# Attention's first four blocks normalized after the value product, first sequence scored from plain float32, half the filler products

## The chip, the core and the metric

The program runs on one core of a Trainium2 chip. Its metric is the device time of one execution in microseconds (us). The core has five engines with a queue each: PE (TensorE, matrix products), ACT (ScalarE), DVE (VectorE), POOL (GpSimd) and SP (SyncE, which here only issues transfers). An engine takes its instructions in the order in which the compiler has put them and waits on semaphores for the others. PE's loading of the stationary operand is listed apart, as PEld.

## The reference

Three stages in float32, each fed by the one before:

```
# attention: B=2 sequences, H=8 heads, S=768 tokens, D=64; 4 sink tokens, window 128
scores = q @ k.T / sqrt(D)
keep   = (key is one of the first n_sink) | (0 <= query - key < window)
a      = exp(scores - max);  a = a / (sum(a) + 1e-9);  x = a @ v       # 1536 tokens x 512
# gated MLP, d_ff = 1536 (weights given as float64)
g = x @ w_gate;  x = (g / (1 + exp(-g)) * (x @ w_val)) @ w_out
# mixture of 8 experts, top 1, with a skip test
out = x;  for tokens with x @ w_skip > 0:  out += gate * relu(x @ w1[e]) @ w2[e]
```

## The kernel before

The 1536 tokens are 12 blocks of 128 (`n` = 0 to 11; six to a sequence, `i = n % 6`). Attention goes by block and by pair of heads (`pr` = 0 to 3, `j = 4n + pr`), because a query block sees only its own and the previous block of keys, and the four sinks. For each pair:

- `step_a`: PE transposes keys and queries into PSUM (`tqk`), ACT copies them into `kq` as float32r, a reduced float32 that PE multiplies in one go (the high half), and DVE subtracts to get what is missing (the low half, `lo_of`, line 71). On a sequence's first block POOL copies the sinks' keys beside them.
- `step_b`: PE makes the scores of two heads, each from three products (high by high, high by low, low by high, line 276; each head uses its own 64 rows of the array). DVE merges the two key blocks with a predicated copy (line 281), adds the mask and takes the maximum (line 286); ACT does exp with the sums (line 290); DVE adds 1e-9 and inverts (lines 291 and 292); DVE scales one head's probabilities and ACT the other's (line 297, and `act_copy` on line 68). DVE copies out the sinks' columns (`psk`, line 300).
- `step_d`: PE transposes the probabilities, ACT copies them out (`pt`), POOL cuts the two triangles.

For each block, `step_s` transposes the sinks' probabilities (`tsk`) and `step_e` sums values times probabilities in PSUM (`xps`, lines 350 and 358). ACT and DVE then write the result as high and low halves (`xt`), the MLP's input.

The MLP takes groups of four blocks. `mlp` runs over 12 chunks of 128 columns of d_ff: gate and value products (`gv`, line 462), tanh, multiply, and the down product (`acc`, line 474). Its weights come as float64. A transfer brings 512 KB into one of three buffers `st`; ACT and DVE turn it into float32, two operations each (lines 134, 135, 139, 140); ACT, with DVE or POOL, splits it into high and low halves (`ring`). There are 36 such conversions, three to a chunk.

The generator `attention` gives out these steps one by one. The first four blocks are drawn by the loop quoted below; it adds, at each of some 56 pulls, filler products on a dead tile (line 428, bf16, 256 columns) at a low priority, and conversions at a rate of six over the loop. The first four phases of the MLP then draw the remaining blocks between their own pieces: phase 0 (blocks 0 to 3) draws blocks 4 to 7.

```
    while done < GS:
        done = next(at)
        pulls += 1
        filler(2)
        while converted[0] < 6 * pulls // 56:
            convert_w()
```

The order on each engine is not the order of the code: a scheduler in the compiler orders instructions by priority and by its own estimate of when their inputs are ready, so conversions and filler products fall wherever it sees an engine free. PSUM pools bound how far the steps run ahead, two buffers each: `accp` holds the scores of the first four blocks, `attp` the transposed keys and queries, `gvp` the transposed probabilities (and later `gv`), `acqp` the sinks, `xps` and the filler's tile.

Of the kernel before, what the change touches and what calls it, by code (L numbers as in the profile page):

```python
# [8 lines left out]
F32 = mybir.dt.float32  # L9
# [4 lines left out]
ALU = mybir.AluOpType  # L14
# [4 lines left out]
def build(ctx: ExitStack, tc: tile.TileContext, q, k, v, n_sink, window,  # L19
# [14 lines left out]
    GB = 2  # L34
    PHASES = [(0, 0, GS, 0, NFC, 2 * GS), (1, 0, GS, 0, NFC, 3 * GS)]
# [138 lines left out]
    def make_masks():  # L174
        parf = const.tile([P, 4], F32, name="parf")
        pneg = const.tile([P, 2], F32, name="pneg")
        ks = const.tile([P, 4], F32, name="ks")
        kt = const.tile([P, 4], F32, name="kt")
# [45 lines left out]
    kq = {(hl, pr): att.tile([P, PW], F32R, name=f"kq{hl}{pr}") for hl in range(2) for pr in range(NPAIR)}  # L224
    vsk = [None] * B
    prob, psk, pt, xt, skt = {}, {}, {}, {}, {}
# [20 lines left out]

    def step_a(j):

        n, pr = divmod(j, NPAIR)  # L250
        i = n % NBLK
        t = attp.tile([P, 512], F32, tag="att", name="tqk")
        for a, src in enumerate((kb[n], qb[n])):
            nc.tensor.transpose(out=t[:, a * P:(a + 1) * P], in_=src[:, 2 * pr:2 * pr + 2, :].rearrange("p h d -> p (h d)"), identity=ident)
        o = (i % 2) * W
        src = t[:, 0:2 * P].rearrange("p (a f) -> p a f", a=2)
        hi, lo = (two(kq[hl, pr], o, KW - o) for hl in range(2))
        act_copy(hi, src)
        lo_of(lo, src, hi)
        if i == 0:  # L260
            for hl in range(2):
                c_ = nc.gpsimd.tensor_copy(kq[hl, pr][:, P:W], kq[hl, pr].bitcast(F32)[:, 0:4])
                begun.setdefault("POOL", c_.ins)

    def step_b(j):
# [7 lines left out]
        for m, (a, c) in enumerate(((0, 0), (0, 1), (1, 0))):  # L273
            for h in range(2):
                r = slice(64 * h, 64 * h + 64)
                m_ = nc.tensor.matmul(out=ss[h][:, 0:nk], lhsT=kq[a, pr][r, KW:PW], rhs=kq[c, pr][r, 0:nk], start=m == 0, stop=m == 2)
# [7 lines left out]
        st = sm.tile([P, 4], F32, tag="st", name="st", bufs=3)  # L284
        for h in range(2):
            r_ = nc.vector.tensor_tensor_reduce(out=p[:, h], in0=ss[h][:, odd * P:odd * P + W], in1=mk, scale=-0.125, scalar=3.0e38,  # L286
                                           op0=ALU.add, op1=ALU.min, accum_out=st[:, h:h + 1])
            begun.setdefault("DVE", r_.ins)
        for h in range(2):
            nc.scalar.activation(out=p[:, h], in_=p[:, h], func=ACTF.Exp, scale=-1.0, bias=st[:, h:h + 1], accum_out=st[:, 2 + h:3 + h])  # L290
# [50 lines left out]
    def step_e(n):  # L341
# [20 lines left out]
        hi, lo = (xt[g][a][:, :, u * P:(u + 1) * P] for a in range(2))  # L362
        act_copy(hi, x)
# [766 lines left out]
    while done < GS:  # L1130
        done = next(at)
        pulls += 1
        filler(2)
# [72 lines left out]
```

## Time and profile before

| what | value |
|---|---|
| three runs | 633.27, 635.26 and 635.63 us, median 635.26 |
| profiled execution | 634.08 us, of which the span of instructions is 632.3 us |
| busy share of the span | PE 93%, PEld 75%, DVE 71%, ACT 59%, POOL 30% |
| mean granted TensorE clock | 0.978 of 2.4 GHz |

The span is what the trace covers; the rest of an execution lies around it. The shares are means over very different stretches: in the first 73 us attention's first four blocks run with little product work, and from there to the experts at the end the MLP keeps PE filled. PE's share also contains the filler products. The chain that ended last holds only the last transfer and so tells nothing about the stage that the change touches; the stretches have to be looked at one by one.

### The profile page before, as it was taken

How to read it: one execution, taken by the hardware profiler on the slowest of the kernel's cores; microseconds unless marked ns; L12 is line 12 of the kernel's file. 1: busy time of each engine (PE TensorE's matmuls, PEld its weight loads, DVE VectorE, ACT ScalarE, POOL GpSimd, SP SyncE). 2: the span in 40 equal slices, each digit the busy share in tenths (PEclk: the TensorE clock that was granted, in tenths of full speed). 3: DMA queues.
4: the chain of work that ended last, by engine and by line, in shares of the span. 5: the costliest groups of instructions: out<-in, count | busy, mean ns of one | idle time of the engine just before them, and what ended most of it. 6: DMA issues, size and time to landing. Idle time of an engine off the chain costs nothing. (4 is left out here: it accounts for less than half of the span.)

```text
span 632.3 us, 10773 instructions
## 1 busy us (share of the span) xinstructions
PE 590.3 (93%) x3449; PEld 474.3 (75%) x3449; DVE 451.4 (71%) x1149; ACT 370.8 (59%) x872; POOL 191.0 (30%) x279
## 2 busy tenths in 40 slices
PE   5889898899999999999999999999997999999993
PEld 3666676668777877777778999899985777777762
DVE  4999889895555585665654577688747697879961
ACT  5788787786545454544553456657615674856730
POOL 4443254465433041101111030021005343537411
PEclk9889998999999999999999999999998999999997
DMA  8668976653010220100004200022108786978901
GB/s 208 147 186 228 259 215 181 200 168 67 0 35 2 84 51 17 36 5 14 1 0 155 96 30 1 1 87 92 33 35 243 250 259 199 338 223 267 345 2 37
DMA packets 78420, 75.81 MB, mean 120 GB/s; under 512 B 43138, under 2 KB 55426, under 8 KB 78352
## 3 DMA queue, kind: packets, MB, share of 16 engines
q1 hardware_dynamic: 75552, 69.32, 36.5%
q0 software_dynamic: 2512, 5.68, 2.7%
q8 instruction: 31, 0.51, 0.3%
q14 instruction: 37, 0.30, 0.2%
q10 hardware_dynamic: 288, 0.00, 0.0%
HBM read 65.37 MB, written 11.98 MB: 122 GB/s over the span
## 5 line engine op out<-in xcount | busy, mean ns | idle before, releaser
L462 PE MATMUL gv<-xt,ring 128*128 128x512 f32 (+1 forms) x1152 | 226.2, 345 | 1.6 <-ACT xt L68 0.8
L462 PEld LDWEIGHTS gv<-xt,ring 128*128 128x128 f32 x1152 | 176.0, 189 | 27.7 <-ACT xt L68 1.1
L68 ACT ACTIVATE ring<-w 128x512 fp32r<-128x512 f32 x144 | 90.3, 629 | 98.0 <-PE gv L462 70.4
L71 DVE TENSOR_TENSOR ring<-w,ring 128x512 fp32r<-128x512 f32 x108 | 74.6, 692 | 41.6 <-ACT ring L68 41.1
L71 DVE TENSOR_TENSOR w<-stage,w 128x512 fp32r<-128x512 f32 x96 | 87.4, 942 | 9.6 <-ACT w L68 7.5
L474 PE MATMUL acc<-ring,hh 128*128 128x512 f32 x288 | 92.5, 402 | 0.0
L68 ACT ACTIVATE w<-stage 128x512 fp32r<-128x512 f32 x128 | 72.9, 626 | 11.9 <-DMA stage<-in_moe_w_dram 8.7
L71 POOL TENSOR_TENSOR ring<-w,ring 128x512 fp32r<-128x512 f32 x36 | 48.5, 1349 | 54.2 <-ACT ring L68 54.1
L321 POOL TENSOR_SCALAR_AFFINE_SELECT pt<-pt 128x256 f32<-128x256 f32 x40 | 19.8, 495 | 138.1 <-ACT pt L68 138.1
L71 POOL TENSOR_TENSOR w<-stage,w 128x512 fp32r<-128x512 f32 x32 | 46.6, 1459 | 48.6 <-ACT w L68 27.0
L474 PEld LDWEIGHTS acc<-ring,hh 128*128 128x128 f32 x288 | 50.8, 188 | 10.8 <-ACT hh L68 0.6
L474 PE MATMUL acc<-ring,hl 128*128 128x512 f32 x144 | 57.2, 399 | 0.0
L290 ACT ACTIVATE p<-p,st 128x132 f32<-128x132 f32 x96 | 38.3, 400 | 31.1 <-DVE st L286 30.4
L877 PE MATMUL yps<-w,hT 128*128 128x512 f32 x192 | 47.1, 399 | 1.0 <-DVE w L71 0.6
L851 PE MATMUL hps<-w,xh 128*128 128x512 f32 x128 | 43.3, 418 | 0.7 <-issue 0.4
L877 PEld LDWEIGHTS yps<-w,hT 128*128 128x128 f32 x192 | 35.3, 188 | 10.4 <-ACTq L925 1.0
L497 DVE TENSOR_TENSOR th<-th,gv 128x512 f32<-128x512 f32 (+1 forms) x48 | 26.5, 552 | 20.7 <-PE gv L462 18.7
L645 POOL DMA_INDIRECT xs<-x,pi x12 | 13.2, 1103 | 81.2 <-ACT ring L68 48.6
L68 ACT ACTIVATE hh<-th 128x512 fp32r<-128x512 f32 (+1 forms) x48 | 25.1, 523 | 16.2 <-DVE th L497 15.7
L496 DVE SCALAR_TENSOR_TENSOR th<-th,gv 128x512 f32<-128x512 f32 (+1 forms) x48 | 26.3, 548 | 8.6 <-ACT th L493 8.6
L474 PEld LDWEIGHTS acc<-ring,hl 128*128 128x128 f32 x144 | 27.0, 188 | 7.0 <-DVE hl L501 0.4
L140 DVE SCALAR_TENSOR_TENSOR w<-w,st 128x512 int32<-128x512 int32 x36 | 30.8, 856 | 1.4
(171 smaller groups left out, 972.2 us busy)
## 6 DMA issues: line engine op xcount, KB each, us to landing
stage<-in_moe_w_dram SPq DMA_DIRECT2D x128, 256.0 KB, 4.5
st<-in_moe_w_gate_dram SPq DMA_DIRECT2D x12, 512.0 KB, 5.6
st<-in_moe_w_val_dram SPq DMA_DIRECT2D x12, 512.0 KB, 4.1
st<-in_moe_w_out_dram SPq DMA_DIRECT2D x12, 512.0 KB, 5.5
xs<-trash SPq DMA_DIRECT2D x8, 387.0 KB
qk<-in_k_dram SPq DMA_DIRECT2D x12, 256.0 KB, 3.9
qk<-in_q_dram SPq DMA_DIRECT2D x12, 256.0 KB, 3.7
vb<-in_v_dram SPq DMA_DIRECT2D x12, 256.0 KB, 3.7
```

The source lines that it names most:

```text
L68: nc.scalar.activation(out=out, in_=in_, func=ACTF.Copy, scale=scale)
L71: (eng or nc.vector).tensor_tensor(out=out, in0=in_, in1=hi.bitcast(F32), op=ALU.subtract)
L140: nc.vector.scalar_tensor_tensor(out=di, in0=di, scalar=3, in1=low, op0=ALU.logical_shift_left, op1=ALU.bitwise_or)
L290: nc.scalar.activation(out=p[:, h], in_=p[:, h], func=ACTF.Exp, scale=-1.0, bias=st[:, h:h + 1], accum_out=st[:, 2 + h:3 + h])
L321: nc.gpsimd.affine_select(out=d[:, 0], in_=d[:, 1], compare_op=ALU.is_ge, fill=0.0, base=0, pattern=[[0, 2], [1, P]], channel_multiplier=-1)
L462: nc.tensor.matmul(out=ps, lhsT=w_[:, kk * P:(kk + 1) * P], rhs=x_[:, kk, t0 * P:t1 * P], start=kk == 0 and m == 0, stop=kk == KD - 1 and ...
L474: nc.tensor.matmul(out=acc[g, t], lhsT=h_[:, s], rhs=w_, start=c == 0 and m == 0, stop=c == NFC - 1 and m == 2)
L496: nc.vector.scalar_tensor_tensor(out=th, in0=th, scalar=1.0, in1=gp, op0=ALU.add, op1=ALU.mult)
L497: nc.vector.tensor_tensor(out=th, in0=th, in1=vp, op=ALU.mult)
L645: d = nc.gpsimd.indirect_dma_start(out=xs[:, :], out_offset=bass.IndirectOffsetOnAxis(ap=pi[:, t], axis=0), in_=x2s[t], in_offset=None, bo ...
L851: nc.tensor.matmul(out=ps[half], lhsT=x_[:, kk, :], rhs=w_[:, kk, :], start=kk == 0 and m == 0, stop=kk == KD - 1 and m == 2)
L877: nc.tensor.matmul(out=y, lhsT=h_[:, c, :], rhs=w_[:, c % 4, :], start=c == 0 and m == 0, stop=c == NF2 - 1 and m == 2)
```

## The change

For blocks 0 to 3 (`n < LATE_SUM`) the probabilities stay unscaled. The sums of all heads of a block go into one tile, which DVE inverts once, after the last pair. In `step_e` PE spreads the inverses over 64 rows each (eight float32 products by the identity, `rps`, in a `gvp` buffer), ACT copies them out (`rs`), and DVE multiplies the block's result by them before it is split into halves. For blocks 0 to 5 (`whole(n)`, the first sequence) ACT's copy of keys and queries keeps full float32, there is no low half, and each head's scores are one float32 product. The loop for the first four blocks adds one filler product a pull. Four small constant tiles become one.

```diff
@@ make_masks @@
-        parf = const.tile([P, 4], F32, name="parf")
...
+        small = const.tile([P, 14], F32, name="small")
+        parf, ks, kt, pneg = small[:, 0:4], small[:, 4:8], small[:, 8:12], small[:, 12:14]
@@ step_a @@
+        if i == 0 and n <= NBLK:
+            new_kq(pr, [F32] if whole(n) else [F32R, F32R])
...
-        hi, lo = (two(kq[hl, pr], o, KW - o) for hl in range(2))
-        act_copy(hi, src)
-        lo_of(lo, src, hi)
+        if whole(n):
+            act_copy(two(kq[0, pr], o, KW - o), src)
+        else:
+            hi, lo = (two(kq[hl, pr], o, KW - o) for hl in range(2))
+            act_copy(hi, src)
+            lo_of(lo, src, hi)
@@ new @@
+    def invert(s):
+        nc.vector.tensor_scalar(out=s, in0=s, scalar1=1e-9, scalar2=None, op0=ALU.add)
+        nc.vector.reciprocal(out=s, in_=s)
@@ step_b @@
-        for m, (a, c) in enumerate(((0, 0), (0, 1), (1, 0))):
+        terms = ((0, 0),) if whole(n) else ((0, 0), (0, 1), (1, 0))
+        for m, (a, c) in enumerate(terms):
...
+        if n < LATE_SUM:
+            if pr == 0:
+                sums[n] = sm.tile([P, H], F32, tag="sums", name="sums")
+            su = sums[n][:, 2 * pr:2 * pr + 2]
+        else:
+            su = st[:, 2:4]
...
-        nc.vector.tensor_scalar(out=st[:, 2:4], in0=st[:, 2:4], scalar1=1e-9, scalar2=None, op0=ALU.add)
-        nc.vector.reciprocal(out=st[:, 2:4], in_=st[:, 2:4])
-        for h in range(2):
-            if h:
-                act_copy(p[:, h], p[:, h], st[:, 2 + h:3 + h])
-            else:
-                nc.vector.tensor_scalar(out=p[:, h], in0=p[:, h], scalar1=st[:, 2 + h:3 + h], scalar2=None, op0=ALU.mult)
+        if n >= LATE_SUM:
+            invert(su)
+            for h in range(2):
...
+        elif pr == NPAIR - 1:
+            invert(sums[n])
@@ step_e @@
+        if n < LATE_SUM:
+            r = gvp.tile([P, NPAIR, P], F32, tag="gv", name="rps")
+            inv = sums.pop(n)
+            for pr in range(NPAIR):
+                for h in range(2):
+                    nc.tensor.matmul(out=r[64 * h:64 * h + 64, pr], lhsT=inv[:, 2 * pr + h:2 * pr + h + 1].to_broadcast([P, D]), rhs=ident, start=True, stop=True, skip_group_check=True)
+            rs = mo.tile([P, RW], F32, tag="x2", name="rs", bufs=4)[:, 0:DM].rearrange("p (a f) -> p a f", a=NPAIR)
+            act_copy(rs, r)
...
+        if n < LATE_SUM:
+            nc.vector.tensor_tensor(out=rs, in0=x, in1=rs, op=ALU.mult)
+            x = rs
         act_copy(hi, x)
         lo_of(lo, x, hi)
@@ the loop for the first four blocks @@
-        filler(2)
+        filler(1)
```

On PE, at the end of block 1 (`s` are the scores, `kq` the transposed keys and queries, `tsk` the sinks' transposition), before:

```order
L276 MATMUL s_638<-kq_118 128x260
L276 MATMUL s_638<-kq_122,kq_118 128x260
L276 MATMUL s_639<-kq_118 128x260
L276 MATMUL s_639<-kq_122,kq_118 128x260
L276 MATMUL s_638<-kq_118,kq_122 128x260
L276 MATMUL s_639<-kq_118,kq_122 128x260
L428 LDWEIGHTS ident
L428 MATMUL warm<-ident 128x256
L254 MATMUL tqk<-ident,qk 128x128
L333 MATMUL tsk<-ident,ps 96x128
```

and at the same place on PE with the change:

```order
L386 MATMUL rps<-ident,sums 64x128
L296 MATMUL s_534<-kq_164 128x260
L296 MATMUL s_535<-kq_164 128x260
L386 MATMUL rps<-ident,sums 64x128 x2
L361 MATMUL tsk<-ident,ps 96x128
L386 MATMUL rps<-ident,sums 64x128 x5
L342 MATMUL tpt<-ident,p 128x128 x2
```

Six score products have become two, and the eight products that spread the inverses stand around them and the sinks' transposition.

On DVE, where the last of the first four blocks is handed to the MLP (`xt` are the MLP's input halves, `st` and `w` a weight under conversion), before:

```order
L300 COPY psk<-p 128x8
L139 SCALAR_TENSOR_TENSOR st<-st 128x512
L281 COPY_PREDICATED s_1152<-above,s_1152 128x128
L140 SCALAR_TENSOR_TENSOR w_100<-w_100,st 128x4x128
L71 TENSOR_TENSOR xt_471<-xps,xt_470 128x4x128
L71 TENSOR_TENSOR kq_124<-tqk,kq_120 128x2x128
```

and with the change:

```order
L401 TENSOR_TENSOR rs<-xps,rs 128x512
L328 COPY psk<-p 128x8
L141 SCALAR_TENSOR_TENSOR st<-st 128x512
L73 TENSOR_TENSOR xt_404<-rs,xt_403 128x4x128
L301 COPY_PREDICATED s_988<-above,s_988 128x128
L142 SCALAR_TENSOR_TENSOR w_98<-w_98,st 128x512
```

The multiplication by the inverses stands ahead of the low half, with a conversion's first step between them; the next pair's low half (`kq`) is gone.

## Rows read from the trace of the kernel before

**Rows 1.** Busy time by stretch: us, busy (x instructions), granted clock, DMA share, GB/s
```profile
9.70:73.10 63.40, 54.60 (x428) 40.77 (x427) 58.65 (x253) 53.05 (x167) 24.77 (x43) 0.92 0.76 204
73.10:143.20 70.10, 63.95 (x320) 48.73 (x321) 61.59 (x139) 53.85 (x125) 35.32 (x42) 0.98 0.67 194
150.00:600.00 450.00, 440.47 (x2545) 361.38 (x2544) 311.43 (x713) 250.53 (x554) 116.74 (x160) 0.99 0.32 103
```
**Rows 2.** PE's waits from 73.1 to 143.2: total us, times, longest
```profile
PE tpt L314 <- DVE st L286: 3.7, 3, 1.7
PE s L276 <- DVE kq L71: 2.1, 2, 1.5
```
**Rows 3.** DVE by line and form, 9.7 to 73.1: count, busy us, mean ns, idle before
```profile
L139 DVE SCALAR_TENSOR_TENSOR st<-st 128x512 int32<-128x512 int32 x14 | 10.5, 750 | 0.1
L140 DVE SCALAR_TENSOR_TENSOR w<-w,st 128x512 int32<-128x512 int32 x14 | 9.6, 685 | 0.2
L71 DVE TENSOR_TENSOR kq<-tqk,kq 128x256 fp32r<-128x256 f32 x17 | 6.9, 416 | 0.1
...
L297 DVE TENSOR_SCALAR p<-p,st 128x132 f32<-128x132 f32 x18 | 6.3, 351 | 0.0
...
L71 DVE TENSOR_TENSOR xt<-xps,xt 128x512 fp32r<-128x512 f32 x3 | 2.0, 682 | 0.0
```
**Rows 4.** DVE in order of time: start, us, instruction
```profile
66.27 0.16 DVE L291 TENSOR_SCALAR st<-st 128x2 f32<-128x2 f32 x1
66.34 0.42 DVE L71 TENSOR_TENSOR kq<-tqk,kq 128x256 fp32r<-128x256 f32 x1
66.68 0.16 DVE L300 COPY psk<-p 128x8 f32<-128x8 f32 x1
...
67.00 0.28 DVE L297 TENSOR_SCALAR p<-p,st 128x132 f32<-128x132 f32 x1
67.19 0.17 DVE L330 CAST ps<-psk 128x32 fp32r<-128x32 f32 x1
```
**Rows 5.** ACT by line and form, 9.7 to 73.1
```profile
L134 ACT ACTIVATE st<-st 128x512 int32<-128x512 uint16 x14 | 9.5, 678 | 1.5 <-DMA st<-in_moe_w_gate_dram 1.2 <-DMA st<-in_moe_w_val_dram 0.4
L135 ACT ACTIVATE w<-st 128x512 f32<-128x512 f32 x14 | 9.4, 672 | 0.0
L68 ACT ACTIVATE p<-p,st 128x132 f32<-128x132 f32 x18 | 7.2, 401 | 2.9 <-DVE st L292 2.1 <-DVE first L551 0.4 <-DVE kt L202 0.4
...
L68 ACT ACTIVATE xt<-xps 128x512 fp32r<-128x512 f32 x4 | 2.4, 588 | 0.0
```
**Rows 6.** PE in order of time, 52 to 75 us
```profile
56.75 1.97 PE L358 MATMUL xps<-pt,vb 128*64 128x128 f32 x32
58.65 0.44 PE L314 MATMUL tpt<-ident,p 128*128 128x128 f32 x2
59.02 0.39 PE L276 MATMUL s<-kq 64*128 64x260 f32 x2
59.24 0.41 PE L276 MATMUL s<-kq,kq 64*128 64x260 f32 x4
59.58 0.44 PE L314 MATMUL tpt<-ident,p 128*128 128x128 f32 x2
...
62.61 0.83 PE L428 MATMUL warm<-ident 128*128 128x256 bf16 x6
...
73.12 0.73 PE L462 MATMUL gv<-xt,ring 128*128 128x512 f32 x2 [0.84 <-ACT xt L68]
```
**Rows 7.** DMA issues: count, KB each, us to landing
```profile
st<-in_moe_w_gate_dram SPq DMA_DIRECT2D x12, 512.0 KB, 5.6
...
xs<-trash SPq DMA_DIRECT2D x8, 387.0 KB
```
**Rows 8.** Busy time and granted clock, two neighbouring stretches of 3 us
```profile
39.00:42.00 3.00, 1.70 (x10) 1.26 (x11) 3.00 (x14) 1.00 (x5) 2.10 (x4) 0.87 1.11 310
42.00:45.00 3.00, 3.00 (x27) 2.82 (x27) 3.00 (x8) 3.00 (x11) 1.59 (x1) 0.56 0.30 96
```

More of the change, by code (lines that the diff above doesn't have):

```diff
@@ L34, in build @@
     GB = 2
+    LATE_SUM = 4
     PHASES = [(0, 0, GS, 0, NFC, 2 * GS), (1, 0, GS, 0, NFC, 3 * GS)]
@@ L223, in build, with new_kq @@
     begun = {}
-    kq = {(hl, pr): att.tile([P, PW], F32R, name=f"kq{hl}{pr}") for hl in range(2) for pr in range(NPAIR)}
+    kq = {}
+    def new_kq(pr, parts):
+        for hl in range(len(parts)):
+            kq[hl, pr] = att.tile([P, PW], parts[hl], tag=f"kq{hl}{pr}", name=f"kq{hl}{pr}")
     vsk = [None] * B
-    prob, psk, pt, xt, skt = {}, {}, {}, {}, {}
+    prob, psk, pt, xt, skt, sums = {}, {}, {}, {}, {}, {}
     def load_sinks(b):
@@ L246, in two, with whole @@
         return bass.AP(a.tensor, a.offset, [a.ap[0], [step, 2], [1, P]])
+    def whole(n):
+        return n < NBLK
     def step_a(j):
@@ L256, in step_a @@
         src = t[:, 0:2 * P].rearrange("p (a f) -> p a f", a=2)
-        hi, lo = (two(kq[hl, pr], o, KW - o) for hl in range(2))
-        act_copy(hi, src)
-        lo_of(lo, src, hi)
+        if whole(n):
[4 more added lines that the diff above has]
+            lo_of(lo, src, hi)
         if i == 0:
-            for hl in range(2):
-                c_ = nc.gpsimd.tensor_copy(kq[hl, pr][:, P:W], kq[hl, pr].bitcast(F32)[:, 0:4])
+            for hl in range(1 if whole(n) else 2):
+                c_ = nc.gpsimd.tensor_copy(kq[hl, pr][:, P:W], (kq[hl, pr] if whole(n) else kq[hl, pr].bitcast(F32))[:, 0:4])
                 begun.setdefault("POOL", c_.ins)
+    def invert(s):
+        nc.vector.tensor_scalar(out=s, in0=s, scalar1=1e-9, scalar2=None, op0=ALU.add)
+        nc.vector.reciprocal(out=s, in_=s)
     def step_b(j):
@@ L272, in step_b @@
         ss = [pool.tile([P, 512], F32, tag=tag, name=f"s{h}") for h in range(2)]
-        for m, (a, c) in enumerate(((0, 0), (0, 1), (1, 0))):
+        terms = ((0, 0),) if whole(n) else ((0, 0), (0, 1), (1, 0))
+        for m, (a, c) in enumerate(terms):
             for h in range(2):
                 r = slice(64 * h, 64 * h + 64)
-                m_ = nc.tensor.matmul(out=ss[h][:, 0:nk], lhsT=kq[a, pr][r, KW:PW], rhs=kq[c, pr][r, 0:nk], start=m == 0, stop=m == 2)
+                x_, y_ = kq[a, pr][r, KW:PW], kq[c, pr][r, 0:nk]
+                m_ = nc.tensor.matmul(out=ss[h][:, 0:nk], lhsT=x_, rhs=y_, start=m == 0, stop=m == len(terms) - 1)
         pe_last[:] = [m_.ins]
@@ L289, in step_b @@
         for h in range(2):
-            nc.scalar.activation(out=p[:, h], in_=p[:, h], func=ACTF.Exp, scale=-1.0, bias=st[:, h:h + 1], accum_out=st[:, 2 + h:3 + h])
-        nc.vector.tensor_scalar(out=st[:, 2:4], in0=st[:, 2:4], scalar1=1e-9, scalar2=None, op0=ALU.add)
-        nc.vector.reciprocal(out=st[:, 2:4], in_=st[:, 2:4])
-        for h in range(2):
-            if h:
-                act_copy(p[:, h], p[:, h], st[:, 2 + h:3 + h])
-            else:
-                nc.vector.tensor_scalar(out=p[:, h], in0=p[:, h], scalar1=st[:, 2 + h:3 + h], scalar2=None, op0=ALU.mult)
+            nc.scalar.activation(out=p[:, h], in_=p[:, h], func=ACTF.Exp, scale=-1.0, bias=st[:, h:h + 1], accum_out=su[:, h:h + 1])
+        if n >= LATE_SUM:
+            invert(su)
+            for h in range(2):
+                if h:
+                    act_copy(p[:, h], p[:, h], su[:, h:h + 1])
+                else:
+                    nc.vector.tensor_scalar(out=p[:, h], in0=p[:, h], scalar1=su[:, h:h + 1], scalar2=None, op0=ALU.mult)
+        elif pr == NPAIR - 1:
+            invert(sums[n])
         if pr == 0:
```

3 lines of the change are left out of this document (removed).

## The prediction

> **What bounds the kernel now.** I read the busy time by stretch first, because the page's shares are means over stages with different limits. [rows 1] has three stages. From 9.70 to 73.10 us attention's first four blocks run: DVE is busy 58.65 of 63.40 us (92.5%), ACT 53.05 (84%), PE 54.60 with its filler products in it. From 73.10 to 143.20 the MLP's first chunks share the engines with blocks 4 to 7 and most weight conversions: PE is busy 63.95 of 70.10, DVE 61.59 (88%). From 150 to 600 PE is busy 440.47 of 450 us. So the first stage goes at DVE's pace, the second is PE's with holes, and the rest is PE's alone. The reader is to see that the MLP's first product, at 73.12 [rows 6], is the event to watch: whatever brings it forward brings the end forward, as far as the second stage doesn't give it back. The view of PE's waits says what the second stage's holes are: score transposes and products that wait for DVE, 3.7 and 2.1 us [rows 2].
>
> The lines of DVE and ACT in the first stage [rows 3, 5] give the work that goes. Their durations overlap a little with the next instruction's, so a price is taken from start to start where DVE is not waiting [rows 4]: a low half 0.34 us (66.34 to 66.68), a scaling of 132 columns 0.19 (67.00 to 67.19), an addition on two columns 0.07 (66.27 to 66.34). For operations of 512 columns I take the mean less the 0.08 us by which the low half's 0.42 exceeds its 0.34.
>
> **DVE in the first stage.** Removed: 17 low halves of keys and queries, 17 x 0.34 = 5.8. Scalings: by the order 18 stand before the MLP's first DVE work and now 3, so 15 go, at 0.19 = 2.9, and of the time by which the 18 are longer than the 0.28 of an undisturbed one (18 x 0.351 - 18 x 0.28 = 1.3) their share, 1.1. Additions and reciprocals: 18 of each become 7 of each, 22 x 0.07 = 1.5. Added: four multiplications of a block by its inverses, 512 columns out of PSUM like the block's low half, 4 x 0.60 = 2.4 [rows 3]. Net -8.9 us. Besides, the order has 13 conversions ahead of that point where it had 15; two of them cost DVE 2 x (0.67 + 0.60) = 2.5, which is put off, not saved. DVE's work falls from 58.65 to 47.2 us.
>
> **ACT in the first stage.** Removed: 16 scalings (18 before, 2 now, by the order) at 0.401 less the same overlap, 16 x 0.32 = 5.1. Added: four copies of the inverses, 4 x 0.51 = 2.0, by the block's copy of the same shape. Put off: two conversions, 2 x (0.60 + 0.59) = 2.4 [rows 5]. ACT falls from 53.05 to 47.6 us, and is then as loaded as DVE.
>
> **How long the first stage gets.** If either engine could be filled as DVE was, to 92.5%, 47.6 us of work take 51.5. If two queues that feed each other fill no better than ACT did, to 84%, they take 56.7. A chain that is now shorter (exp goes straight to the transpose, without addition, reciprocal and scaling) speaks for the first, the fact that two engines are level for the second; I take the middle, 54.1 instead of 63.4. At the last block the multiplication comes between the products and ACT's high half, +0.6. The MLP's first product comes 9.3 - 0.6 = 8.7 us earlier, at about 64.4; bounds 6.1 and 11.3. The low half of that block now stands behind the first step of a conversion, which waits for its 512 KB and ACT. Behind it wait the MLP's second kind of product (high by low) and the next block's predicated copies. In the order of before a conversion's second step stood there, so I add nothing; if its transfer is late it costs up to its landing time, 5.6 us [rows 7].
>
> **PE in the first stage** hides its part. The six score products of a pair take 59.58 - 59.02 = 0.56 us for 260 columns. How fast a float32 product goes is seen on line 358: 16 by the order (32 records) in 58.65 - 56.75 = 1.90 us, 0.119 each for 128 columns [rows 6]. Two score products of 260 columns are 0.48 us by that; 0.24 if the two heads, on their own 64 rows, run side by side on top of it; 0.97 if line 358, which writes to two halves of the output, is already side by side and the heads' rows are not. I take 0.48, the row as it stands. The 32 products that spread the inverses cost 32 x 0.119 = 3.8 us; 59 fewer filler products by the order give back 59 x 0.11 = 6.5 (six in 0.83 us, of which some 0.27 is one product's way through). PE is lighter than before, so this moves nothing as long as its clock holds.
>
> The Trainium skill bears on the float32 product: its page "FP8 and Floating Point Precision", section "TensorE Precision Notes", says that true float32 takes four passes through the array. By an estimate from that page at 2.4 GHz, 260 columns are 0.43 us a head, 0.43 for a pair side by side and 0.87 one after the other, so that the pair would cost -0.13 or +0.31 us against 0.56. The row of 0.119 us for 128 columns is less than four passes one after another (0.21), so here either the halves run side by side or the passes are fewer.
>
> **The second stage.** Of the low halves still made in it, four (block 5) go, 4 x 0.34 = 1.4; the two put-off conversions come in, 2.5. DVE has 1.1 us more, and since PE's holes there are DVE's, I count it whole: +1.1. Eight pairs of blocks 4 and 5 have two score products for six, 8 x (0.48 - 0.56) = -0.6; bounds -2.6 and +3.3. Transfers: in SP's order before, six of the eight clears (`xs`, 387 KB) stand ahead of the 15th weight; now none does ahead of the 16th. The stage moved 194 GB/s x 70.1 us = 13.6 MB; six clears and two weights more make 17.0 MB, 243 GB/s. The stretch at 39 us shows 310 [rows 8], so it fits; but weights queue behind clears, and a conversion blocks ACT while it waits for its transfer. I take +0.7 us, bounds 0 and 3. From 150 us on nothing is changed, and a shift passes through PE's full queue whole.
>
> **The sum.** -8.7 + 1.1 - 0.6 + 0.7 = -7.5 us on the profiled execution of 634.08 (632.3 of span and 1.8 around it): 626.6. That execution lies 1.2 under the median of the runs, so the forecast is 635.26 - 7.5 = 627.8. Its own range, from 6.1 or 11.3 and the other bounds partly together, is 623 to 631.
>
> **Rivals.**
>
> *The float32 products run one after the other, at 0.97 a pair.* For it: nothing in the trace shows two float32 products on different rows of the array. Against: the six float32r products take 0.56 us, where 260 columns at one a cycle of 2.4 GHz are 0.108 each and 0.65 in turn, so there the heads' rows do overlap. The first stage still hides it; the second pays 3.3 instead of -0.6: 635.26 - 3.6 = 631.7.
>
> *The start is earlier but the weights aren't.* The MLP begins at 64 with two conversions fewer, 3.4 MB more to move, and DVE and ACT still 85% busy with conversions. If its chunks then wait for weights, most of the 8.7 comes back as PE waiting for `ring`. For it: ACT's conversions wait for DMA already [rows 5]. Against: those waits are short, and PE's waits in the second stage name no weight [rows 2]. With 2 us left: 633.3.
>
> *The clock falls.* Filler products are there while PE has little else, and half of them go. The trace shows the low level of 1.2 GHz after sparse stretches: from 42 to 45 us the mean granted clock is 0.56, after 39 to 42 with PE busy 1.70 of 3 us [rows 8]. In the new order a pair costs PE at the full clock about 0.48 for scores, 0.7 for the two kinds of transposes (0.37 for two, from 58.65 to 59.02), 0.9 as its part of the block's products and the spread inverses, 0.4 filler: 2.5, or 40 us for 16 pairs. At the low level for a share x of that work it is 40 x (1 + x). It passes the 63.4 us of before at x = 0.6, and from there on PE, not DVE, sets the stage; at x = 0.8 the MLP starts 9 us later than 73, and with a chunk's beginning at the low level, but fewer holes after it, the kernel takes 635.26 + 6 = 641. Against: 0.92 is the stage's mean now, PE loses net only a few of its 54.6 busy us while the stage gets shorter by more, and a PE that becomes the bound is busy, which in the trace is where the clock is full.
>
> On this the Trainium skill's page "TensorE: Matmul & The Clock Gate", Part 1, states that the throttled clock is the default and that activity releases it. The trace agrees: 1.70 of 3 us busy is followed by 0.56, and the filled stage from 150 us has 0.99 [rows 1, 8].
>
> *The change doesn't do what it says* has no chance of its own: the order shows the products, low halves and scalings gone.
>
> **How the numbers follow.** My forecast 0.58, the serial float32 products 0.12, the gain given back 0.18, the clock 0.12. A difference of under 0.5% (3.2 us, so 632.1 to 638.4) can't be told from no change here. Of the forecast nearly all is faster, of the serial case most, of the given-back case a quarter: 0.58 + 0.09 + 0.05, and 0.02 for what lies in between, 0.74 faster; 0.15 same; 0.11 slower, nearly all of it the clock. The range leaves out the clock's far end and the best corner: 622.5 to 636.
>
> **What would show each step.** In the changed profile: the first `gv` product near 64 us (at 73 or later the first stage is wrong); DVE's busy time up to there near 47 us and its share beside ACT's (a DVE at 92% with ACT at 84% would mean that I took too little off); the start-to-start time of two score products, 0.24, 0.48 or 0.97; PE's waits in the 70 us after the start, near 6 us (if over 12, or if they name `ring` or a transfer, the second rival); the granted clock of the first stage, 0.92 before (under 0.65 with PE full, the third). Wrong altogether would be a start 8 us earlier and an end that isn't, without any of these waits.

## The result and the profile after

| | before | after |
|---|---|---|
| median of the runs on one chip | 634.57 us (19 runs, 632.3 to 639.95) | 629.96 us (19 runs, 625.97 to 634.3) |
| ratio, 95% interval | 1 | 0.9917 [0.9893, 0.9941] |
| profiled execution, span | 634.08, 632.3 us | 628.07, 626.3 us |
| first `gv` product | 73.12 us | 65.23 us |
| eighth tanh of the MLP | 157.63 us | 153.52 us |

The changed kernel is faster by 4.6 us, where 7.5 was forecast. The last two lines of the table say where the difference arose: the first stage gave back 7.89 us (8.7 forecast), and the second stage, counted here from the first `gv` product to the eighth tanh, took 88.29 us instead of 84.51, 3.8 us more (1.2 forecast). What was gained by the eighth tanh, 4.1 us, goes through to the experts unchanged; the MLP's last product starts 4.3 us earlier, and the stretch behind it varies by 2.5 us among the fourteen profiles.

Busy time by stretch of the kernel after, columns as in [rows 1]:

```profile
9.70:65.23 55.53, 53.54 (x397) 35.79 (x396) 45.56 (x195) 46.68 (x151) 28.22 (x46) 0.94 0.68 175
65.23:135.33 70.10, 63.52 (x295) 46.38 (x295) 58.52 (x129) 51.88 (x122) 33.65 (x42) 0.95 0.77 225
150.00:600.00 450.00, 440.69 (x2544) 361.98 (x2545) 316.19 (x719) 253.88 (x561) 116.40 (x159) 0.99 0.32 102
```

DVE's busy time fell from 58.65 to 45.56 us and ACT's from 53.05 to 46.68. PE's hardly moved, 54.60 to 53.54, in a stage that is 8 us shorter: it is now busy for 96% of it, where DVE has 82% and ACT 84%. That alone doesn't make PE the bound, because busy time runs to a product's modelled end (a filler by itself counts 0.27 us, six in a row take 0.83 [rows 6]), so that short pauses hide in it; the experiments have to say. DVE's lines of the same stretch, as in [rows 3], show in the last column that DVE now waits for PE:

```profile
L312 DVE CUSTOM_DVE_ANT_0 p<-s,mask 128x132 f32<-128x132 f32 x36 | 9.4, 286 | 3.2 <-PE s L296 3.0
L142 DVE SCALAR_TENSOR_TENSOR w<-w,st 128x512 int32<-128x512 int32 x11 | 8.8, 796 | 1.1 <-ACT w L137 1.0
L141 DVE SCALAR_TENSOR_TENSOR st<-st 128x512 int32<-128x512 int32 x12 | 8.4, 707 | 0.5 <-ACT st L136 0.4
L301 DVE COPY_PREDICATED s<-above,s 128x128 f32<-128x128 int32 x28 | 7.6, 289 | 4.0 <-PE s L296 3.8
L73 DVE TENSOR_TENSOR xt<-rs,xt 128x512 fp32r<-128x512 f32 x4 | 3.7, 924 | 0.5 <-ACT xt L70 0.4
...
L401 DVE TENSOR_TENSOR rs<-xps,rs 128x512 f32<-128x512 f32 x4 | 2.8, 688 | 1.6 <-PE xps L395 1.5
```

The 17 low halves `kq` of [rows 3] are gone and the 18 scalings are two (0.7 us). DVE idles 8.3 us for PE's scores and value products, which it hardly did before. PE's own waits, first up to the first `gv` product, then in the 70.1 us after it, as in [rows 2]:

```profile
PE tsk L361 <- DVE ps L73: 0.9, 1, 0.9
PE rps L386 <- ACT st L136: 0.6, 1, 0.6
PE s L296 <- DVE st L312: 0.3, 1, 0.3
```

```profile
PE tpt L342 <- DVE st L312: 3.8, 3, 2.2
PE s L296 <- ACT pt L70: 1.4, 1, 1.4
PE acc L514 <- POOL ring L73: 0.6, 1, 0.6
PE acc L514 <- ACT ring L70: 0.4, 1, 0.4
PE tqk L265 <- DVE st L312: 0.3, 1, 0.3
```

1.8 us of waits in the first stage. In the second they are 6.5 us. Before, they were 7.0, of which 0.84 lie ahead of the first product [rows 6], so 6.2: of the stage's extra 3.8 us the waits explain 0.3. The rest is in PE's busy time, as the whole second stages show, of the kernel before, of the kernel after, and of two of the experiments below, the changed kernel once more (e6) and the changed kernel without fillers (e5):

```profile
73.12:157.63 84.51, 78.38 (x415) 60.29 (x416) 69.94 (x161) 62.02 (x146) 44.49 (x51) 0.98 0.61 173
```

```profile
65.23:153.52 88.29, 81.71 (x408) 60.51 (x408) 73.74 (x161) 64.43 (x151) 45.23 (x53) 0.96 0.70 202
```

```profile
63.89:149.62 85.73, 79.78 (x408) 59.41 (x408) 73.70 (x161) 64.30 (x152) 45.93 (x52) 0.98 0.72 208
```

```profile
68.62:150.50 81.88, 77.88 (x405) 58.15 (x405) 71.33 (x164) 64.59 (x152) 46.86 (x53) 1.00 0.75 218
```

PE's busy time (second number) goes with the granted clock (the third from the end): 77.88 us at 1.00, 79.78 at 0.98, 81.71 at 0.96, for the same products of the MLP. What is left to the length of the stage are the waits, 4.0, 5.8 and 6.5 us. Four more kernels below have a full clock in this stage (e1, e2, e9, e11); their PE is busy for 77.2 to 77.4 us of it.

### The profile page after: what moved, and what is told of

It reads as the page before. It is cut to its first block, busy times and chain, and to the rows that moved or that the text cites. A ratio compares the mean times of both kernels' runs of the same rounds, so it can differ in the third digit from the quotient of the medians.

```text
span 626.3 us, 10603 instructions
## 1 busy us (share of the span) xinstructions
PE 591.7 (94%) x3408; PEld 469.2 (75%) x3408; DVE 442.2 (71%) x1089; ACT 367.2 (59%) x860; POOL 193.7 (31%) x275
## 5 line engine op out<-in xcount | busy, mean ns | idle before, releaser
L73 POOL TENSOR_TENSOR ring<-w,ring 128x512 fp32r<-128x512 f32 x36 | 49.8, 1385 | 55.4 <-ACT ring L70 47.9
L349 POOL TENSOR_SCALAR_AFFINE_SELECT pt<-pt 128x256 f32<-128x256 f32 x40 | 22.4, 560 | 125.7 <-ACT pt L70 125.7
L685 POOL DMA_INDIRECT xs<-x,pi x12 | 13.3, 1104 | 81.2 <-ACT ring L70 48.6
L296 PE MATMUL s<-kq 64*128 64x260 f32 (+1 forms) x144 | 36.6, 412 | 1.8 <-ACT pt L70 1.4
L301 DVE COPY_PREDICATED s<-above,s 128x128 f32<-128x128 int32 x80 | 21.6, 290 | 18.5 <-PE s L296 18.2
```

Of the source, the lines that this page charges most:

```text
L73: (eng or nc.vector).tensor_tensor(out=out, in0=in_, in1=hi.bitcast(F32), op=ALU.subtract)
L296: m_ = nc.tensor.matmul(out=ss[h][:, 0:nk], lhsT=x_, rhs=y_, start=m == 0, stop=m == len(terms) - 1)
L301: nc.vector.copy_predicated(ss[h][:, odd * W:odd * W + P], above, ss[h][:, (1 - odd) * W:(1 - odd) * W + P])
L349: nc.gpsimd.affine_select(out=d[:, 0], in_=d[:, 1], compare_op=ALU.is_ge, fill=0.0, base=0, pattern=[[0, 2], [1, P]], channel_multiplier=-1)
L685: d = nc.gpsimd.indirect_dma_start(out=xs[:, :], out_offset=bass.IndirectOffsetOnAxis(ap=pi[:, t], axis=0), in_=x2s[t], in_offset=None, bo ...
```

## Experiments

Twelve runs were made, in three lots, each lot on one chip with runs of the kernel before (medians 634.2 to 634.4). All of them in one table; "start" is the first `gv` product and "second" the time from it to the eighth tanh, both from each kernel's profiled execution, and "clock" the mean granted clock up to the start.

| kernel | late sums | float32 scores | filler a pull | start | clock | second | ratio, 95% interval |
|---|---|---|---|---|---|---|---|
| before | no | no | 2 | 73.12 | 0.92 | 84.51 | 1 |
| after | yes | yes | 1 | 65.23 | 0.94 | 88.29 | 0.9917 [0.9893, 0.9941] |
| e6, the same again | yes | yes | 1 | 63.89 | 1.00 | 85.73 | 0.9881 [0.9831, 0.9931] |
| e3 | no | no | 1 | 78.47 | 0.75 | 84.93 | 1.0029 [0.9998, 1.006] |
| e2 | no | yes | 1 | 69.51 | 0.86 | 86.77 | 0.9970 [0.9940, 0.9999] |
| e10 | yes | no | 2, placed nearer | 75.36 | 0.99 | 87.31 | 1.0042 [1.0018, 1.0066] |
| e7 | yes | yes | 2, placed nearer | 77.12 | 1.00 | 84.18 | 1.0021 [0.9994, 1.0048] |
| e4 | yes | yes | 2, half of them late | 67.66 | 1.00 | 101.62 | 1.0027 [0.9986, 1.0067] |
| e1 | yes | no | 1 | 64.07 | 0.91 | 82.64 | 0.9862 [0.9806, 0.9917] |
| e12, e1 again | yes | no | 1 | 65.39 | 1.00 | 86.26 | 0.9875 [0.984, 0.9911] |
| e5 | yes | yes | 0 | 68.62 | 0.91 | 81.88 | 0.9829 [0.9785, 0.9872] |
| e11, e5 again | yes | yes | 0 | 72.25 | 0.75 | 81.72 | 0.9872 [0.9831, 0.9913] |
| e9 | yes | no | 0 | 73.01 | 0.87 | 82.26 | 0.9963 [0.9939, 0.9988] |
| e8 | yes | one float32r product | 1 | 64.11 | 0.97 | 86.95 | 0.9825 [0.9779, 0.987] |

### First lot: which part carries the gain (e1 to e4)

**e1**: late normalization and half the filler, scores as before.

```diff
     def whole(n):
-        return n < NBLK
+        return False
```

> The change without the float32 scores: late normalization and one filler product a pull, scores again from three products with low halves. The MLP's first gv product was at 73.1 us before and at 65.2 with the whole change. DVE theory (the prediction's): DVE has 17 low halves more, 5.8 us, and sets the first stage: start at 69 to 71, DVE over 90% busy up to there. PE theory (with the whole change PE is the new wall of the first stage, since its busy time is 53.5 of 55.5 us there): a pair's scores cost 0.56 instead of 0.64 on PE, so the start stays at 64 to 66.

Measured: 626.73 us (6 runs), ratio 0.9862, start 64.07. The low halves of keys and queries are back on DVE (49.28 us busy to the start, against 45.56), and nothing is lost by it: what the float32 scores took off DVE was not on the path. The start is the one that the expectation gave for PE as the wall (64 to 66); DVE's share, 91% here and 88% in e12, is the one it gave for DVE, so e1 by itself doesn't name the wall.

**e2**: float32 scores and half the filler, normalization as before.

```diff
-    LATE_SUM = 4
+    LATE_SUM = 0
```

> The change without the late normalization: float32 scores for the first sequence, one filler product a pull, probabilities scaled pair by pair as before. DVE theory: DVE keeps the scalings, additions and reciprocals (5.5 us) and loses the block multiplications (2.4), ACT keeps 16 scalings: start at 67 to 69. PE theory: PE is spared the 32 products that spread the inverses (3.8 to 7.6 us by the trace of the whole change), so the start is at 63 to 66.

Measured: 633.32 us (10 runs), ratio 0.9970, start 69.51 and a second stage of 86.77. A gain of 0.3%, by its interval 0.6 at most: of the 7.9 us at the start it reaches 3.6, and the second stage gives back 2.3, with PE idle for 9.6 us of it. The start fits neither reading of the expectation (67 to 69, 63 to 66); the clock up to it, 0.86, was in neither.

**e3**: the kernel before with half the filler.

```diff
-        filler(2)
+        filler(1)
```

> The kernel before with one filler product a pull instead of two, nothing else. If filler products are hidden and the clock holds: start at 73 +- 0.7 and the time unchanged within 0.3%. If they hold up the products behind them in PE's queue: start at 70 to 72, time 0.2 to 0.4% shorter. If the clock falls: mean granted clock of the first stage under 0.87 and the start at 74 to 76.

Measured: 637.32 us (10 runs), ratio 1.0029, start 78.47, 5.35 us later than before. Its stretch up to the start:

```profile
9.70:78.47 68.77, 59.77 (x372) 43.54 (x371) 55.57 (x247) 52.29 (x164) 25.23 (x43) 0.75 0.67 175
```

Five us more than before in the stage, and DVE is less busy, not more: the granted clock is 0.75 instead of 0.92, and PE is busy for 59.77 us where it was for 54.60 with twice the filler [rows 1]. So the forecast's third rival is a mechanism of this kernel: with normalization as it was, half the filler is too little to hold the clock. One profile would not show that, but the ten timed runs do: over the whole span their clock is 0.966 in the mean, against 0.978 in the 25 runs of the kernel before beside them. It did not decide in the changed kernel, where the clock is 0.94 and 1.00.

**e4**: the changed kernel with two filler products a pull, as before.

```diff
-        filler(1)
+        filler(2)
```

> The whole change with two filler products a pull as before. DVE theory: PE has room, start at 65.2 +- 0.7. PE theory: some 55 filler products more at 0.11 us are 6 us on the wall, of which the warmer clock (mean 0.94 to perhaps 0.99) gives back 1 to 2: start at 68 to 71 and the time 0.4 to 0.8% over that of the whole change.

Measured: 637.38 us (10 runs), ratio 1.0027. It did not test what it was made for. The scheduler put 59 of the low-priority products behind the MLP's first product (65 stand ahead of it, 75 behind; 124 and 16 in the kernel before), where they take 9.9 us of PE's time clear of waits (from each product's start to the next one's, less the wait in between) and 13.3 with them. The second stage took 101.62 us; its clock is also low from 130 to 145 us (0.73, 0.50 and 0.74), so not all of that is the fillers' own. With as many fillers ahead of it as in the changed kernel the start is 67.66, and PE is busy for 55.78 us up to there against e6's 50.54 at the same full clock: another order of the same products can cost that much.

### Second lot: the fillers, the same program again, and the price of float32 (e5 to e8)

**e5**: the changed kernel without filler in the loop.

```diff
-        filler(1)
+        filler(0)
```

> The whole change without any filler product. Its MLP started at 65.2 us with one a pull; the kernel before with one a pull instead of two had a mean granted clock of 0.75 in the first stage (0.92 with two) and started 5.4 us later. Clock theory: the clock of the first stage falls from 0.94 to 0.65 to 0.8 and the start moves to 68 to 74. PE-wall theory: 55 filler products at 0.11 us are 6 us off the wall, the float32 products alone keep the clock up: start at 60 to 64.

Measured: 625.69 us (4 runs), ratio 0.9829. The start is later, 68.62, with the clock down to 0.50 from 60 to 65 us; but the second stage takes 81.88, at a clock of 1.00 all through, as its row above shows, so that the whole is no slower than the changed kernel. The start lies in the range of the expectation's clock reading (68 to 74), the mean clock, 0.91, above its 0.65 to 0.8; e11 has 72.25 at 0.75. The other reading, 60 to 64, is out: the fillers do work for the clock.

**e6**: the changed kernel, nothing edited.

> The whole change once more, as a control for what two profiles of one program differ by. If the stages are settled by the order of the instructions: start within 0.7 us of 65.2, the eighth tanh within 1 us of 153.5. If the moments at which the clock falls are chance: the second stage (88.3 us) differs by 2 us or more with another clock than 0.95.

Measured: 627.67 us (4 runs), ratio 0.9881; in its profiled execution the start is 63.89 and the second stage 85.73, in all 3.9 us less than in the first profile of the same program. So the expectation's second reading holds: order alone doesn't settle the stages. Here the two can be laid side by side. PE in order of time in the first profile of the changed kernel, then in this one (the bracket is the wait before the instruction):

```profile
19.01 0.40 PE L386 MATMUL rps<-ident,sums 128*64 128x128 f32 x2 [0.62 <-ACT st L136]
...
21.32 0.45 PE L361 MATMUL tsk<-ident,ps 128*96 128x128 f32 x1 [0.89 <-DVE ps L73]
21.70 1.54 PE L386 MATMUL rps<-ident,sums 128*64 128x128 f32 x10
```

```profile
19.23 0.40 PE L386 MATMUL rps<-ident,sums 128*64 128x128 f32 x2 [0.63 <-ACT st L136]
...
21.54 0.31 PE L361 MATMUL tsk<-ident,ps 128*96 128x128 f32 x1 [0.88 <-DVE ps L73]
21.78 0.87 PE L386 MATMUL rps<-ident,sums 128*64 128x128 f32 x10
```

The same instructions behind the same waits, 0.62 and 0.89 against 0.63 and 0.88 us, and the ten records behind them take 1.54 us in the one and 0.87 in the other. The stretches around it, first profile and this one:

```profile
15.00:20.00 5.00, 4.38 (x33) 2.73 (x31) 4.42 (x21) 4.92 (x21) 2.41 (x3) 1.00 0.98 231
20.00:25.00 5.00, 4.11 (x28) 3.20 (x28) 4.85 (x16) 3.12 (x9) 3.01 (x3) 0.64 0.76 188
25.00:30.00 5.00, 5.00 (x34) 3.21 (x31) 2.78 (x10) 2.75 (x9) 1.65 (x4) 0.68 0.80 184
```

```profile
15.00:20.00 5.00, 4.37 (x35) 2.94 (x32) 4.42 (x23) 4.82 (x20) 2.19 (x3) 1.00 1.03 234
20.00:25.00 5.00, 4.12 (x45) 2.83 (x41) 5.00 (x14) 3.70 (x13) 3.21 (x3) 1.00 0.71 178
25.00:30.00 5.00, 3.66 (x28) 2.53 (x26) 4.62 (x19) 3.75 (x13) 2.83 (x6) 1.00 0.85 194
```

In the second stage the first profile has two falls of the clock (0.67 from 105 and 0.66 from 130 us), this one a single fall (0.66 from 125). Around 105 us, first profile and this one:

```profile
100.00:105.00 5.00, 3.60 (x18) 2.52 (x17) 4.51 (x8) 3.67 (x8) 0.82 (x1) 1.00 1.01 288
105.00:110.00 5.00, 4.39 (x14) 3.07 (x12) 3.66 (x13) 2.75 (x8) 2.49 (x5) 0.67 1.08 285
```

```profile
100.00:105.00 5.00, 3.03 (x15) 1.79 (x14) 4.05 (x10) 3.01 (x9) 2.49 (x3) 1.00 1.07 242
105.00:110.00 5.00, 5.00 (x25) 3.58 (x23) 2.43 (x7) 3.37 (x10) 2.37 (x5) 1.00 0.72 232
```

The stretch with the emptier PE, 3.03 of 5 us, is the one that is not followed by a fall. The second stage's 2.6 us are the clock's by the rows shown with the result: PE's busy time there differs by 1.9 and its waits by 0.7. Of the start's 1.3 us this is less sure, since e1 starts at 64.07 with a fall of the clock early in the stage (0.50 from 15 to 20 us) and e12, the same program, at 65.39 without one.

**e7**: as e4, with the filler products at a priority nearer to that of the work around them, so that all stay ahead of the MLP's first product (124 and 16, as before).

```diff
-        tc.cur_priority = p + 1000
+        tc.cur_priority = p + 50
...
-        filler(1)
+        filler(2)
```

> The whole change with two filler products a pull, at a priority near the code's place (50 behind it instead of 1000), so that by the order none of them stands behind the MLP's first product (59 did in the version with two). Spill theory: that version lost its 11 us in the second stage because those 59 stood there; now the second stage is back to 84 to 89 us. The first stage takes the fillers: start at 66 to 71, so the time is between 627 and 635. If the spilled products were not the cause, the second stage stays over 95 us.

Measured: 636.42 us (10 runs), ratio 1.0021. The second stage, 84.18, is the one expected if the late fillers were e4's loss; the start and the time lie above the expected 71 and 635. The clock is full up to the start, which is 77.12, 13.2 us later than e6's at the same clock. The stretch, and DVE's two main waits in it:

```profile
9.70:77.12 67.42, 65.49 (x449) 41.87 (x448) 50.35 (x196) 52.25 (x154) 26.44 (x45) 1.00 0.71 184
```

```profile
L312 DVE CUSTOM_DVE_ANT_0 p<-s,mask 128x132 f32<-128x132 f32 x34 | 8.9, 284 | 5.5 <-PE s L296 5.5
L301 DVE COPY_PREDICATED s<-above,s 128x128 f32<-128x128 int32 x28 | 7.9, 290 | 4.2 <-PE s L296 4.2
```

PE is busy for 97% and DVE waits 9.7 us for its scores. ACT is busy for 77%. With the whole change and as many fillers as before, DVE and ACT wait for a PE that has no room, and the gain is gone. Two things changed besides the count: the fillers' priority, and with the order the conversions ahead of the start (16 or 17 where e6 has 11 or 12). The kernel before with its fillers at the nearer priority was not run, so the fillers' own share of the 13.2 us isn't known.

**e8**: the scores of the first sequence from one float32r product instead of one float32 product; the low parts are left out there. (A second line of the edit fits POOL's copy of the sinks' keys to the new type.)

```diff
-            new_kq(pr, [F32] if whole(n) else [F32R, F32R])
+            new_kq(pr, [F32R] if whole(n) else [F32R, F32R])
```

> The whole change with each score product of the first sequence taken in float32r instead of float32 (the low parts are left out of the scores there). A pair's scores cost PE 0.2 us or less instead of 0.64, and nothing else changes. If the float32 products are what holds the first stage now: start at 60 to 63 and a shorter second stage, 84 to 86. If the first stage hides them: start at 65 +- 0.7.

Measured: 624.84 us (4 runs), ratio 0.9825; start 64.11, within 0.3 us of e6's. The time's interval overlaps e6's, so all that can be said of it is that float32 products cost at most some 6 us over the cheapest product there is. The start says more. Up to it:

```profile
9.70:64.11 54.41, 50.71 (x363) 34.67 (x362) 42.93 (x192) 45.87 (x149) 27.24 (x47) 0.97 0.71 176
```

Clear of waits the scores take PE 10.2 us here and 16.6 in e6. The 6.3 us that PE is spared bring the start no nearer, though DVE and ACT have less to do as well, and PE's busy time stays where it was (50.71 and 50.54), because its other products are counted longer, with short pauses in them. A fall of the clock from 55 to 60 us (0.66; an estimate from it is 1.7 us of work lost) hides a part of it at most. So with half the filler PE is not alone the wall: no room for more work is not the same as a gain from less.

### Third lot: late normalization alone, and the two best again (e9 to e12)

**e9**: e1 without filler in the loop (`filler(0)`).

> Late normalization alone, and no filler products in the loop for the first four blocks (10 remain ahead of the MLP's first product, from elsewhere). Theory A (with the change PE itself is the first stage's wall, and filler products are work on it that nothing needs): about 20 fewer low-halves are gone from DVE than in the whole change, but PE has least work of all versions; the MLP's first product near 66 us, second stage near 82, ratio to before 0.984, level with the version without fillers that has float32 scores (0.983) and with late normalization plus half the fillers (0.986). Theory B (the clock decides: fewer fillers, lower clock): first stage's granted clock under 0.80, the first product after 72 us, ratio 1.00 or more.

Measured: 631.93 us (12 runs), ratio 0.9963. The start is 73.01: neither theory's numbers, but B's direction. The clock holds until 35 us and then falls twice:

```profile
35.00:40.00 5.00, 4.14 (x25) 2.99 (x25) 4.44 (x26) 2.67 (x11) 0.81 (x2) 0.61 0.78 200
...
55.00:60.00 5.00, 5.00 (x39) 4.34 (x38) 2.03 (x6) 2.55 (x7) 1.26 (x1) 0.50 0.27 70
```

**e10**: late normalization alone, the fillers as before (e1 with the two edits of e7).

> Late normalization alone, with all filler products as before (124 ahead of the MLP's first product, as in the kernel before). Theory A (PE is the wall once DVE's work is gone): the clock is full (1.00) and PE is busy to over 95% of the first stage; the first product near 75 us, like the 77.12 of the whole change with all fillers, and ratio 1.000: late normalization brings its gain only where fillers go with it. Theory B (PE hides its part, as the forecast had it): the first product near 65 us and ratio 0.986, like late normalization with half the fillers.

Measured: 637.02 us (12 runs), ratio 1.0042, start 75.36: theory A's numbers and not B's. Its stretch, and the last 5.66 us of it:

```profile
9.70:75.36 65.66, 58.37 (x489) 43.19 (x489) 58.64 (x215) 52.25 (x157) 30.76 (x49) 0.99 0.73 192
...
69.70:75.36 5.66, 2.44 (x27) 1.66 (x24) 3.83 (x11) 3.32 (x9) 0.91 (x3) 0.87 0.92 243
```

A's reason is not confirmed by it. PE is busy for 89%, not 95, DVE for as much, and DVE has 58.64 us to do, as in the kernel before (58.65 [rows 1]): a stage set by DVE, as the forecast had it, would be as long. The reason is in DVE's lines:

```profile
L142 DVE SCALAR_TENSOR_TENSOR w<-w,st 128x512 int32<-128x512 int32 x16 | 14.2, 894 | 0.3 <-ACT w L137 0.2
L141 DVE SCALAR_TENSOR_TENSOR st<-st 128x512 int32<-128x512 int32 x16 | 11.3, 710 | 0.6 <-ACT st L136 0.6
```

With all fillers in PE's queue 16 conversions stand ahead of the start, as in e7; with half of them 11 or 12 (the kernel after, e12). So fillers go with two costs: e10's 57 more take PE 7.7 us more than e12's, clear of waits (16.2 against 8.5), and some 4 more conversions come in on DVE and ACT, 25.5 us on DVE's two lines against 16.2. A third came by the order. The last block's products end at 70.8 us, but ACT's copy of its result stands behind a conversion whose weight is late:

```profile
74.14 0.65 ACT L136 ACTIVATE st<-st 128x512 int32<-128x512 uint16 x1 [1.71 <-DMA st<-in_moe_w_val_dram]
74.70 0.61 ACT L70 ACTIVATE xt<-rs 128x512 fp32r<-128x512 f32 x1
...
75.36 0.79 PE L502 MATMUL gv<-xt,ring 128*128 128x512 f32 x1 [2.44 <-ACT xt L70]
```

From the start of the last of these products to the first `gv` product e10 takes 4.9 us, where the other kernels take 1.7 to 2.9. The forecast named this risk for DVE's low half, behind a conversion's first step. So e10 does not show that PE was in the way; for that there is e7.

**e11**: e5 again. **e12**: e1 again.

> The whole change without filler products once more. If its first profile (first product at 68.62 with a fall of the clock ahead of it, second stage 81.9) was typical, the ratio is 0.983 again and lies below that of the change (0.990). If the small number of timed runs flattered it, the ratio is 0.990 and the two are level.

> Late normalization with half the filler products and the scores as before, once more. First reading 0.986, first product at 64.07 us. Theory A (late normalization carries the gain, float32 scores add nothing to it): 0.986 again, level with or below the whole change's 0.990. Rival (the float32 scores add some 2 us that the first reading's execution hid): 0.993.

Measured: 626.25 us (6 runs, 0.9872) for e11, between the two readings of its expectation, and 626.19 us (6 runs, 0.9875) for e12, theory A. Both of these kernels beat the kernel before in both lots. That they also beat the changed kernel is likely but not shown. Only e5 was measured beside it, in e6's lot, 625.69 against 627.67 us with four runs each, and the intervals overlap. Over all lots e1 and e12 have a median of 626.4 us in 12 runs, e5 and e11 625.7 in 10, the changed kernel and e6 629.8 in 23; drawing from these runs again and again puts the first difference at 1.6 to 5.7 us and the second at 2.0 to 5.5, but across chips.

## Why the prediction was right in its size and incomplete in its reason

**DVE's and ACT's work.** Forecast 47.2 and 47.6 us; measured 45.56 and 46.68 (46.33 and 46.92 in e6). The counts held: 17 low halves and 16 of the 18 scalings went. The new multiplication takes 0.69 us, near the row of [rows 3] it was priced by. One price was missed: the block's low half now reads `rs` instead of `xps` and takes 0.92 us in the mean instead of 0.68, at 0.69 in e12 and 0.99 in e9.

**The start.** Forecast 64.4, bounds 61.8 to 67.0; measured 65.23, and 63.89 in e6. Right.

**"PE hides its part."** This is the step that failed. The forecast let DVE and ACT set the stage and put three terms on PE, cheaper scores, the spread inverses and 6.5 us given back by half the filler, which made it lighter in sum and were to move nothing. PE's waits are 1.8 of 55.5 us, and it has no room: in e7, the same change with as many fillers as before ahead of the start and some conversions more, the start is 77.12, with PE busy for 97% and DVE waiting for it. The two edits need each other: half the filler alone is 1.0029 (the clock falls), late normalization with all fillers 1.0042 (more conversions and a late weight, with the fillers in PE's queue), late normalization with half of them 0.9862. What is not shown is that PE alone sets the changed kernel's first stage. e8 spares it 6.3 us and starts no sooner, and ACT is busy for 84 to 87% of the stage in the changed kernel, e6, e1, e12 and e8, within the forecast's 84 to 92.5. For the kernel as changed the forecast's account by ACT and DVE is not refuted; it is its "this moves nothing" that is.

The size came right by some luck: PE's three terms were all off, and most of it cancels. Clear of waits, from the kernel before (mean clock 0.92) to e6 (1.00), the scores grew by 0.9 us where the forecast's prices make them smaller, the spread inverses added 6.0 for 3.8, and the fillers gave back 9.2 for 6.5:

- A filler product was priced at 0.11 us, by six in a row [rows 6]. Spread among other work it takes 0.13 to 0.15 us clear of waits (7.1 us for 55 records in e6, 17.5 for 114 in e7); the kernel before has 16.3 us for its 114, so the row in a stream was not the one to take.
- The 32 products that spread the inverses take 6.7 us, 6.0 in e6, not 3.8; in a row they go at the price taken (8 in 1.02 us in e12), but the order cuts them into pieces (the rows of e6 above), and the block that meets the low clock pays 1.5 us for five.
- A pair of scores takes 0.64 us, not 0.48, and more where the order puts other work between its heads. PE in e6, four pieces in order of time:

```profile
13.57 0.49 PE L296 MATMUL s<-kq 64*128 64x132 f32 x2
13.99 0.33 PE L342 MATMUL tpt<-ident,p 128*128 128x128 f32 x1
...
16.84 0.71 PE L296 MATMUL s<-kq 64*128 64x260 f32 x4
17.48 0.33 PE L342 MATMUL tpt<-ident,p 128*128 128x128 f32 x1
```

```profile
52.33 0.70 PE L296 MATMUL s<-kq 64*128 64x260 f32 x2
52.96 0.33 PE L342 MATMUL tpt<-ident,p 128*128 128x128 f32 x1
53.13 0.38 PE L468 MATMUL warm<-ident 128*128 128x256 bf16 x2
53.45 0.47 PE L296 MATMUL s<-kq 64*128 64x260 f32 x1
```

A float32 product shows as two records. One head of 260 columns takes 52.96 - 52.33 = 0.63 us, both heads one behind the other 17.48 - 16.84 = 0.64: the heads' rows do work side by side, and the serial rival (0.97) is out. One head of 132 columns takes 0.42. The difference, 0.21 us for 128 columns, is 1.64 ns a column, and 0.20 us remains that does not depend on the columns. The forecast took a price from a row of products in a stream, which holds neither the 0.20 nor the case of a head by itself. In the second half of the first stage most pairs are cut in two by a filler or a transpose, so that a pair takes 2 x 0.63. The mean in e6 is 0.95 a pair (13.8 us for 29 products), close to the serial rival's 0.97, though not by its mechanism. At 1.64 ns a column 128 columns are 0.21 us, so the 0.119 of line 358 [rows 6] was already two halves side by side, which the forecast's price left open. The Trainium skill's page "FP8 and Floating Point Precision", section "TensorE Precision Notes", counts four passes for true float32; an estimate by it is 4 / 2.4 GHz = 1.67 ns a column, and the 1.64 read here agrees.

**The second stage.** Forecast +1.2 us; measured +3.8, and +1.2 in e6, the same program. The agreement in e6 does not confirm the terms: the scores of 260 columns in it take 4.7 us where they took 4.1, so +0.7 and not -0.6; transfers went to 225 GB/s, not 243; PE's waits for `ring` are 1.0 us, near the 0.7 taken, but all waits together rose by 0.3 where DVE's part alone was to add 1.1. By the rows of the result the stage would take about 77.9 + 6.5 = 84.4 us at a full clock, as long as before. The term that the sum lacked is the clock in this stage: PE's busy time above 77.9 us is 3.8 us in the first profile, with two falls of the clock, 1.9 in e6, with one, and 0.5 in the kernel before, which has one too (0.66 from 105 us). The 77.9 is e5's; by the 77.2 to 77.4 of the other four each of these is some 0.6 more.

**The rivals.** Serial float32: out, by the rows above. Weights late: PE's waits of the second stage name `ring` for 1.0 us and no transfer, well below what would give the gain back. The clock: true of the kernel before (e3), not of the change, whose 19 runs have 0.984 in the mean over the span where the kernel before has 0.978 to 0.980 beside the three lots. What no rival held is that PE has no room left at a full clock.

**The total.** 629.96 us lies 2.2 above the forecast 627.8 and inside its own range, 623 to 631; e6, 627.67, lies on it. The falls of the clock, which the forecast had only as a rival of the first stage, come in some executions of the second and not in others, and so belong in the sum as a cost with a spread. What remains open is what sets the changed kernel's first stage, PE's queue or ACT's, and why the whole change's float32 scores help without fillers (e5 and e11 against e9) and, if anything, cost with them (e6 against e12): that a float32 product keeps PE busy for longer, as a filler would, fits the clock's rows but was not tested apart.

## What to carry to other kernels

When one engine's work is cut, look at the queue of the next engine for what stood there only because it had time: taking half the fillers away gained nothing while DVE set the pace, and cutting DVE's work gained nothing while all the fillers stayed; only both edits together did. Test a suspected bound from both sides, with more work on it and with less, since a queue without room for more need not be the only bound. Price an operation from a row in which it stands as it will stand in the new order (alone, in a pair, in a stream), since the part that doesn't depend on its size shows in the first and not in the last. Profile the same program twice before explaining a few us of difference, and count fillers and conversions ahead of the event in every version, because a scheduler may move them.

## What the runs showed of the hardware

- The granted clock fell at 21 us in one execution and stayed full in another of the same program, behind waits of PE that agree within 0.01 us (0.62 and 0.89 us).
- A float32 product on 64 rows takes 0.42 us for 132 columns and 0.63 for 260, and a second head on the other 64 rows adds 0.01 us when it follows at once.
- DVE's low half of 128x512 took 0.68 us from PSUM [rows 3], and 0.69 to 0.99 us in the mean from the two operands in SBUF. What sets which was not tried.
- The kernels without filler (e5, e11) reach 0.983 and 0.987 with starts of 68.6 and 72.3 us: both had a low clock ahead of the MLP and none in the second stage, 82 us long instead of 86 to 88. Why the clock holds there in them, and in e9, and falls in the changed kernel, no run here tells.
